# The hidden layer of batches 2 to 7 by seven block products, and attention beside the out layer

## The chip, the cores and the metric

One core of one Trainium2 chip runs the kernel. The metric is device time in microseconds (us); the median of three runs of the kernel before is 381.51 us (381.17 to 381.83). TensorE is called PE here, VectorE DVE, ScalarE ACT, GpSimd POOL and SyncE SP, as in the profile.

## What is computed

```
q, k, v: [8 batches, 12 heads, 448 rows, 64]
scores = q @ k^T / 8 - log(448);  attn = sigmoid(scores);  y = attn @ v
x = y with the heads side by side: [8*448, 768]
h = x @ w_in          (w_in  [768, 2048])
g = h * sigmoid(h)    (this is silu)
out = g @ w_out       (w_out [2048, 768]), float32 [3584, 768]
```

## The kernel before

Matmuls take float16 and add up in PSUM; q, k, v and the weights are cast by POOL's loads.

**Attention.** A *quad* `g` holds four heads of a batch, so a batch is three quads and there are 24. A quad has seven *chunks*; a `(g, ch)` pair is a unit, 168 in all (`units`). `scores` (L169) issues four 64x64 matmuls into a `pssc` tile, and one ACT sigmoid over 128x896 writes `attnT`. There are two `pssc` tiles of two PSUM banks each. `values` (L193) multiplies a quad's seven `attnT` tiles by v (seven *rounds* of four matmuls) and DVE writes the two halves into `xT[b]`, scaled by 64.

**Hidden layer.** `h_unit(b, fc)` (L229) is six matmuls of 448 columns for one of 16 blocks of 128 hidden columns; ACT takes the sigmoid and DVE multiplies, into `gTr`, which holds two batches side by side.

**Out layer.** `out_set` (L288) makes the rows of two blocks of 128 columns of `gTr` by a seven-product scheme: seven `product`s of eight matmuls of 384 columns, with sums of weights `tw[1]` to `tw[4]` (made once by `w_sums`, 16 subtractions of 128x768 on DVE, L277) and sums of `gTr` blocks `sg` (DVE, L318 to L327). In order the products read `wq[0][0]`, `wq[1][0]`, `tw[3]`, `tw[2]`, `tw[4]`, `tw[1]`, `wq[1][1]`. A pair of batches has three sets; every second pair has a fourth, made of the seventh block of this pair and of the one before (`kept`).

**PSUM banks.** All other PSUM tiles (`ph`, `po`, `pav`, `ptr`) share the tag `ps1` with four banks. A new tile gets, of the banks that are free at its place in the program, the one that was given back first.

**Order.** The order of instructions is written out by hand. `all_moe` is one generator of matmul steps for the hidden and the out layer, `stream`. The loop at the end (L541) issues two units of scores (a *burst*), a quad's values if any wait, and then calls `stretch(ns)`, which draws that many nanoseconds (189 for a hidden matmul, 163 for an out matmul) from the stream. So PE's queue holds bursts and stretches in turn. Up to unit 41 the stretches are 1,600 ns; at unit 42 there is one of 21,500 ns, in which h of batch 1 ends, and after that 2,000 to 3,400 ns. The last sets and h of batch 7 run after attention has ended.

**Queues.** POOL's queue holds the loads in order of the program: `load("kq", g)` is four DMAs, `load("v", g)` two. `after_values(g)` issues `v` of quad g+3, and others; quad 2 issues v 5, the last halves of `w_out`, kq 6 and kq 7; `transposes(4, "q")` issues kq 8; quad 5 issues kq 9. From quad 6 on, `dma_transpose` (L158) copies rows of k and q into `kr` and `qr` (ACT or DVE) and SP transposes them by DMA; the stores of the results are on SP too. For quads 6, 7, 8 `by_h1` puts these copies behind blocks 3, 6, 9 of h of batch 1, on ACT.

Of the kernel before, what the change touches and what calls it, by code (L numbers as in the profile page):

```python
# [2 lines left out]

# [14 lines left out]
def kernel(  # L18
# [14 lines left out]
    P = 128  # L33
# [88 lines left out]

    def new_qkT(g):
        for name in ("k", "q"):
            qkT[name, g] = p4.tile([P, NCH, P], F16, tag=f"{name}T", name=f"{name}T")

    dummy = cpool.tile([P, 512], F16, tag="dummy", name="dummy")

# [29 lines left out]
    def dma_transpose(g, name, copy):  # L158
        if ("k", g) not in qkT:
            new_qkT(g)  # L160
        rows = p3.tile([P, NCH, 2, D], F16, tag=f"{name}r", name=f"{name}r")
        copy(rows, flat[name, g].rearrange("p j c d -> p c j d"))  # L162
        nc.sync.dma_start_transpose(
            out=qkT[name, g], in_=rows.rearrange("p c j d -> p (c j d)")
        )
# [27 lines left out]
    def values(g, end=NCH):  # L193
        b, iq = divmod(g, NQ)
        if b not in xT:
            assert b < 2 or b - 2 in h_done
            xT[b] = p2.tile([P, NPAIR, S], F16, tag="xT", name="xT")
        pav, done_rounds = part_of.pop(g, None) or (
            [ps_1.tile([P, 512], F32, tag="ps1", name="pav") for _ in range(2)],
            0,  # L200
        )
        for ch in range(done_rounds, end):
            at = attnT.pop((g, ch))
            for half in range(2):
                own = slice(half * HP, (half + 1) * HP)
                for j in range(2):
                    nc.tensor.matmul(  # L207
                        pav[half][j * D : (j + 1) * D, :S],
                        flat["v", g][own, j, ch, :],
                        at[own, j, :],  # L210
                        start=(ch == 0),
                        stop=(ch == NCH - 1),
                    )
        if end < NCH:
            part_of[g] = pav, end
            return
        for half in range(2):
            nc.vector.tensor_scalar_mul(xT[b][:, half * NQ + iq, :], pav[half][:, :S], SX)  # L218
        if iq == NQ - 1:
            ready.add(b)  # L220

# [7 lines left out]
    def h_unit(b, fc):  # L229
        nonlocal hold  # L230
        hold = b > 0 and fc == NFC - 1
        ph = ps_1.tile([P, 512], F32, tag="ps1", name="ph")
        for at, cc in enumerate(pairs):
            assert b in ready or at < 4
            nc.tensor.matmul(  # L235
                ph[:, :S],
                w_in_sb[:, cc, fc * P : (fc + 1) * P],
                xT[b][:, cc, :],
                start=(at == 0),
                stop=(at == NCC - 1),  # L240
            )
            if at < NCC - 1:
                yield 189
        if fc == NFC - 1:
            h_done.add(b)
        tsig = p3.tile([P, S], F16, tag="tsig", name="tsig")
        nc.scalar.activation(tsig, ph[:, :S], AF.Sigmoid, bias=0.0, scale=ISX)  # L247
        nc.vector.tensor_mul(  # L248
            gTr[:, fc, (b % 2) * S : (b % 2) * S + S], ph[:, :S], tsig
        )  # L250
        yield 189

    rows_of = out.rearrange("(b p c) e -> b c p e", b=B, c=NCH)

# [11 lines left out]
    def w_sums():  # L266
        for i in (2, 3, 4):
            tw[i] = cpool.tile([P, NHC, NO2], F16, tag=f"T{i}", name=f"T{i}")
        tw[1] = wq[0][1]
        for o, x, y in (  # L270
            (tw[3], wq[1][1], wq[0][1]),
            (tw[1], wq[0][1], wq[0][0]),
            (tw[2], wq[1][1], tw[1]),
            (tw[4], tw[2], wq[1][0]),
        ):
            for f in range(0, NHC, 2):
                nc.vector.tensor_sub(o[:, f : f + 2], x[:, f : f + 2], y[:, f : f + 2])  # L277
                yield

    kept = cpool.tile([P, NFC, P], F16, tag="kept", name="kept")  # L280
# [4 lines left out]
    def row_blocks(m, g):  # L285
        return [rows_of[2 * m + u // NCH, u % NCH] for u in (2 * g, 2 * g + 1)]

    def out_set(a1, rows1, a2, rows2, last=False):  # L288
        nonlocal hold
        lo, hi = slice(0, NHC), slice(NHC, NFC)  # L290
        osb = [p4.tile([P, DMODEL], F32, tag="osb", name="osb") for _ in range(2)]
        c11, c12 = (osb[0][:, nh * NO2 : (nh + 1) * NO2] for nh in range(2))
        c21, c22 = (osb[1][:, nh * NO2 : (nh + 1) * NO2] for nh in range(2))
        m1 = p2.tile([P, NO2], F32, tag="m1", name="m1")
        sg = [cpool.tile([P, NHC, P], F16, tag=f"S{i}", name=f"S{i}") for i in range(1, 5)]

        def store(rows, o, cols, engines):
            for at, (row, eng) in enumerate(zip(rows, engines)):
# [1 line left out]

        left, right, whole = slice(0, NO2), slice(NO2, DMODEL), slice(0, DMODEL)

        def product(a, w):
            po = ps_1.tile([P, 512], F32, tag="ps1", name="po")
            for fc in range(NHC):
                nc.tensor.matmul(  # L306
                    po[:, :NO2], a[:, fc, :], w[:, fc, :], start=(fc == 0), stop=(fc == NHC - 1)
                )
                if fc < NHC - 1:
                    yield 163  # L310
            return po[:, :NO2]

        def plus(o, po, x, sign=ISX):
            nc.vector.scalar_tensor_tensor(  # L314
                out=o, in0=po, scalar=sign, in1=x, op0=ALU.mult, op1=ALU.add
            )

        nc.vector.tensor_sub(sg[2], a1[:, lo], a2[:, lo])  # L318
        nc.vector.tensor_add(sg[0], a2[:, lo], a2[:, hi])
        po = yield from product(a1[:, lo], wq[0][0])  # L320
        nc.scalar.activation(m1, po, AF.Copy, scale=ISX)  # L321
        nc.vector.tensor_sub(sg[1], sg[0], a1[:, lo])
        hold = False
        yield 163
        po = yield from product(a1[:, hi], wq[1][0])
        plus(c11, po, m1)
        nc.vector.tensor_sub(sg[3], a1[:, hi], sg[1])  # L327
        if last:
            store(rows1, osb[0], left, (nc.sync, nc.sync))
        yield 163  # L330
        po = yield from product(sg[2], tw[3])
        plus(c22, po, m1)
        yield 163
        po = yield from product(sg[1], tw[2])
        plus(c22, po, c22)
        plus(c12, po, m1)
        yield 163
        po = yield from product(a2[:, hi], tw[4])
        plus(c21, po, c22, -ISX)
        yield 163  # L340
        po = yield from product(sg[0], tw[1])
        plus(c22, po, c22)
# [9 lines left out]
        yield 163  # L352


    by_h1 = {3: 6, 6: 7, 9: 8}
    early = [h_unit(0, fc) for fc in range(2)]
    sums = w_sums()

    def moe_h(b):
        for fc in range(NFC):  # L360
            yield from early[fc] if b == 0 and fc < 2 else h_unit(b, fc)
            if b == 1:
                if fc >= 2:
                    next(sums)
                if fc in by_h1:
                    for name in ("k", "q"):
                        dma_transpose(by_h1[fc], name, act_copy)

    def moe_set(m, g):
        step = out_set(block(g), row_blocks(m, g), block(g + 1), row_blocks(m, g + 1))  # L370
        for i, ns in enumerate(step):
            if m % 2 == 0 and g == 2 and i % 8 == 4 and i < 32:
                fcs = slice(i // 8 * 4, i // 8 * 4 + 4)
                nc.scalar.activation(kept[:, fcs], block(NCH - 1)[:, fcs], AF.Copy)
            if m == 0 and g == 0 and i in (10, 14):
                next(sums)
            yield ns

    def all_moe():
        for m in range(B // 2):  # L380
            yield from moe_h(2 * m)
            if m > 0:
                yield from moe_set(m, 0)
            yield from moe_h(2 * m + 1)
            if m == 0:
                yield from moe_set(m, 0)
            yield from moe_set(m, 2)
            yield from moe_set(m, 4)
            if m % 2 == 1:
                g = NCH - 1  # L390
                yield from out_set(
                    kept, row_blocks(m - 1, g), block(g), row_blocks(m, g), m == B // 2 - 1
                )

    stream = all_moe()
# [44 lines left out]
    def after_values(g):  # L440
# [18 lines left out]
                load("kq", to)  # L459
        if g == 5:  # L460
            load("kq", 9)
        if g >= 6 and g + 3 < NQB:
            later.extend(((g + 3, "k"), (g + 3, "q")))

    later = []

    def rows_if_any():
        if later:
            g, name = later.pop(0)
            dma_transpose(g, name, nc.vector.tensor_copy)  # L470
            if name == "q" and g + 4 < NQB and g + 4 > 12:
                load("kq", g + 4)

    def values_if_any():
        if waiting:
            g = waiting.pop(0)
            values(g)
            after_values(g)

    keep_busy(9)  # L480
    pe_transpose(
# [54 lines left out]
        for do, *what in behind.get(n, ()):  # L536
            do(*what)

    paces = {1: 1600, 2: 2000, 3: 2550, 4: 3400, 5: 3400, 6: 3000, 7: 3000}
    stretch(paces[1])  # L540
    for n in range(NT_B + 3, len(units), 2):  # L541
        burst = units[n : n + 2]
        if n == 2 * NT_B:
            values_if_any()
            stretch(21500)
        for u in burst:
            scores(*u)
        values_if_any()
        rows_if_any()
        for g, ch in burst:  # L550
            if ch == NCH - 1:
                waiting.append(g)
        if n in (24, 30):
            transposes(4 + (n - 24) // 6, "k")
        elif n in (26, 32):
            transposes(4 + (n - 26) // 6, "q")
        stretch(paces[1] if 1 not in ready else paces[n // NT_B])
    for g in waiting:
        values(g)
    for _ in stream:  # L560
        pass

# [29 lines left out]
```

## Time and profile before

| | before |
|---|---|
| median of 3 runs | 381.51 us (381.17 to 381.83) |
| the profiled execution | 381.95 us, its span 380.2 us |
| PE busy | 370.8 us, 98% of the span |
| DVE, ACT, POOL busy | 235.2, 225.9, 93.5 us |
| granted TensorE clock | 1.000 |
| hidden matmuls (L235) | 768 |
| out matmuls (L306) | 784 |
| units of scores (L183) | 168, 918 ns each on ACT |

Durations are of the one profiled execution; start times count from the start of its span. "Idle before" is the time in which the engine stood still before an instruction, and what ended it. A matmul's duration contains its latency; what one costs in a row is the distance from start to start, so a group's start and the next group's start give the price.

### The profile page before, as it was taken

How to read it: one execution, taken by the hardware profiler on the slowest of the kernel's cores; microseconds unless marked ns; L12 is line 12 of the kernel's file. 1: busy time of each engine (PE TensorE's matmuls, PEld its weight loads, DVE VectorE, ACT ScalarE, POOL GpSimd, SP SyncE). 2: the span in 40 equal slices, each digit the busy share in tenths (PEclk: the TensorE clock that was granted, in tenths of full speed). 3: DMA queues.
4: the chain of work that ended last, by engine and by line, in shares of the span. 5: the costliest groups of instructions: out<-in, count | busy, mean ns of one | idle time of the engine just before them, and what ended most of it. 6: DMA issues, size and time to landing. Idle time of an engine off the chain costs nothing.

```text
span 380.2 us, 7666 instructions
## 1 busy us (share of the span) xinstructions
PE 370.8 (98%) x3083; PEld 186.0 (49%) x3083; DVE 235.2 (62%) x416; ACT 225.9 (59%) x329; POOL 93.5 (25%) x158
## 2 busy tenths in 40 slices
PE   7989999999999999999999999999999999999995
PEld 2444445545554445445555444544455444555563
DVE  2636646987565666566766647735757446656773
ACT  4988875757667764777434576477764776054000
POOL 8946325403752323122221303101100000000000
PEclk9999999999999999999999999999999999999999
DMA  7999999995999947945939949536347300110233
GB/s 125 177 185 204 205 204 171 133 140 110 165 241 216 151 56 99 173 54 69 162 67 183 132 78 121 71 86 74 48 85 97 84 3 2 50 34 0 82 85 83
DMA packets 66403, 42.80 MB, mean 113 GB/s; under 512 B 37056, under 2 KB 62912, under 8 KB 66368
## 3 DMA queue, kind: packets, MB, share of 16 engines
q0 software_dynamic: 28032, 22.59, 43.2%
q1 hardware_dynamic: 38112, 19.41, 28.5%
q8 instruction: 24, 0.39, 0.4%
q10 hardware_dynamic: 224, 0.33, 0.3%
q14 instruction: 11, 0.09, 0.1%
HBM read 45.61 MB, written 11.01 MB: 149 GB/s over the span
## 4 chain that ended last, share of the span: by engine, by line
PE 78%; DMA 13%; POOL 3%; DVE 3%; ACT 2%; issue 1%; ACTq 0%; POOLq 0%
PE po L306 34%; PE ph L235 29%; PE psc L176 8%; PE pav L207 6%; DMA w_in_sb<-in_moe_w_in_dram 5%; DMA w_out_sb<-in_moe_w_out_dram 5%; DMA qf<-in_q_dram 1%; DMA vf<-in_v_dram 1%; POOL kf L78 1%; DVE gTr L248 1%; DVE T L277 1%; POOL qf L78 1%; ACT qr L137 1%; POOL vf L78 1%; ACT attnT L183 0%
## 5 line engine op out<-in xcount | busy, mean ns | idle before, releaser
L183 ACT ACTIVATE attnT<-psc 128x896 f16<-128x896 f32 x168 | 144.2, 918 | 59.9 <-PE psc L176 59.8
L235 PE MATMUL ph<-xT,w_in_sb 128*128 128x448 f16 x768 | 153.2, 353 | 1.2 <-DMA w_in_sb<-in_moe_w_in_dram 1.2
L248 DVE TENSOR_TENSOR gTr<-ph,tsig 128x448 f16<-128x448 f32 x128 | 78.9, 623 | 70.1 <-ACT tsig L247 68.6
L235 PEld LDWEIGHTS <-w_in_sb 128*128 128x128 f16 x768 | 71.9, 98 | 77.1 <-issue 12.8
L247 ACT ACTIVATE tsig<-ph 128x448 f16<-128x448 f32 x128 | 68.6, 547 | 54.4 <-PE ph L235 53.7
L78 POOL DMA_DIRECT2D vf<-in_v_dram x48 | 28.9, 624 | 136.4 <-PE pav L207 136.4
L306 PEld LDWEIGHTS <-S 128*128 128x128 f16 x448 | 42.3, 98 | 33.9 <-issue 6.8
L314 DVE SCALAR_TENSOR_TENSOR osb<-po,osb 128x384 f32<-128x384 f32 x70 | 37.6, 554 | 25.2 <-PE po L306 24.5
L176 PE MATMUL psc<-qT,kT 64*64 64x448 f16 x672 | 50.7, 362 | 0.9 <-ACT attnT L183 0.3
L218 DVE TENSOR_SCALAR xT<-pav 128x448 f16<-128x448 f32 x48 | 27.7, 619 | 31.4 <-PE pav L207 31.4
L306 PE MATMUL po<-T,S 128*128 128x384 f16 x224 | 40.6, 327 | 0.1
L306 PEld LDWEIGHTS <-gTr 128*128 128x128 f16 x304 | 28.7, 98 | 23.4 <-issue 5.0
L306 PE MATMUL po<-w_out_sb,S 128*128 128x384 f16 x224 | 39.9, 326 | 0.0
L207 PE MATMUL pav<-attnT,vf 64*64 64x448 f16 x672 | 37.5, 349 | 0.2 <-DVE gTr L248 0.2
L78 POOL DMA_DIRECT2D qf<-in_q_dram x46 | 27.7, 613 | 39.4 <-DVE qr L162 16.7
L306 PE MATMUL po<-w_out_sb,gTr 128*128 128x384 f16 x192 | 34.7, 327 | 0.0
L78 POOL DMA_DIRECT2D kf<-in_k_dram x50 | 30.3, 618 | 7.8 <-DVE kr L162 4.3
L176 PEld LDWEIGHTS <-kT 64*64 64x64 f16 x672 | 14.2, 104 | 31.0 <-issue 29.0
L207 PEld LDWEIGHTS <-vf 64*64 64x64 f16 x672 | 20.1, 107 | 12.3 <-issue 1.5
L314 DVE SCALAR_TENSOR_TENSOR osb<-po,m 128x384 f32<-128x384 f32 x42 | 23.1, 551 | 3.9 <-PE po L306 2.5
L306 PE MATMUL po<-T,gTr 128*128 128x384 f16 x112 | 21.4, 326 | 0.0
L321 ACT ACTIVATE m<-po 128x384 f32<-128x384 f32 x14 | 6.9, 492 | 24.0 <-PE po L306 24.0
(41 smaller groups left out, 130.8 us busy)
## 6 DMA issues: line engine op xcount, KB each, us to landing
out_dram<-osb SPq DMA_DIRECT2D x54, 192.0 KB, 3.0
vf<-in_v_dram POOLq DMA_DIRECT2D x48, 112.0 KB, 4.4
kf<-in_k_dram POOLq DMA_DIRECT2D x46, 112.0 KB, 5.4
qf<-in_q_dram POOLq DMA_DIRECT2D x46, 112.0 KB, 5.8
w_in_sb<-in_moe_w_in_dram POOLq DMA_DIRECT2D x4, 768.0 KB, 10.6
w_out_sb<-in_moe_w_out_dram POOLq DMA_DIRECT2D x4, 768.0 KB, 17.1
kT<-kr SPq DMA_TRANSPOSE x18, 5.8
qT<-qr SPq DMA_TRANSPOSE x18, 5.6
```

The lines of the kernel that those rows point to most:

```text
L78: nc.gpsimd.dma_start(flat[name, g][half * HP : (half + 1) * HP, :, c0:c1].rearrange("p i c d -> p i (c d)"), source[name][b, h0 : h0 + 2] ...
L137: nc.scalar.activation(o, i, AF.Copy)
L176: nc.tensor.matmul(psc[own, j, :S], qkT["k", g][rows, ch, own], qkT["q", g][rows, :, own], start=True, stop=True,)
L183: nc.scalar.activation(attnT[g, ch], psc[:, :, :S], AF.Sigmoid, bias=NEG_LOG_S, scale=QKSCALE)
L207: nc.tensor.matmul(pav[half][j * D : (j + 1) * D, :S], flat["v", g][own, j, ch, :], at[own, j, :], start=(ch == 0), stop=(ch == NCH - 1),)
L218: nc.vector.tensor_scalar_mul(xT[b][:, half * NQ + iq, :], pav[half][:, :S], SX)
L235: nc.tensor.matmul(ph[:, :S], w_in_sb[:, cc, fc * P : (fc + 1) * P], xT[b][:, cc, :], start=(at == 0), stop=(at == NCC - 1),)
L247: nc.scalar.activation(tsig, ph[:, :S], AF.Sigmoid, bias=0.0, scale=ISX)
L248: nc.vector.tensor_mul(gTr[:, fc, (b % 2) * S : (b % 2) * S + S], ph[:, :S], tsig)
L306: nc.tensor.matmul(po[:, :NO2], a[:, fc, :], w[:, fc, :], start=(fc == 0), stop=(fc == NHC - 1))
L314: nc.vector.scalar_tensor_tensor(out=o, in0=po, scalar=sign, in1=x, op0=ALU.mult, op1=ALU.add)
L321: nc.scalar.activation(m1, po, AF.Copy, scale=ISX)
```

## The change

For batches 2 to 7 the hidden layer is made per pair of batches (`h_pair`). The two batches' `xT`, each cut into two halves of 384 rows, and `w_in`, cut into four blocks, are multiplied by a scheme of seven block products of three matmuls per 128 hidden columns, in place of eight. For each `i` of eight, products 1 and 2 add up in the bank `xb`, 6, 7 and 4 in `y` (a `pssc` tile), 5 and 3 in `z`; ACT copies product 1 out (`p1`), DVE adds (`u2`, `u3`, `p1`), and ACT takes one `Silu` per sum into `gTr`. Products 3 and 4 of block `i` run inside block `i+1` (`late`). The sums of `w_in` (`w_in_sums`: nine of 128x1024 drawn during h of batch 0, three more in the second out set) and the sums of `w_out` (`w_sums`, 16 of 128x768, drawn during h of batch 1) are made on POOL; the sums of `xT` (`x_sums`) on DVE. Batches 0 and 1 keep `h_unit`.

All units of scores of the next pair are issued in the out layer's time of the pair before; `h_pair` runs with no scores. `Silu` and `Sigmoid` are called on one element (`warm`) where they change. The first set of a later pair does the rest of the last block inside its first product, and reads `tw[3]` second. Buffers: `qkT` 3 (was 4), `rows` 2 (was 3), `osb` 3 (was 4). `gTr` of batches 2 to 7 holds silu itself, so the out sets' factor there is 1.

```
...
-        rows = p3.tile([P, NCH, 2, D], F16, tag=f"{name}r", name=f"{name}r")
+        rows = p2.tile([P, NCH, 2, D], F16, tag=f"{name}r", name=f"{name}r")
...
+            if b > 2 and b % 2 == 1 and iq == NQ - 1 and half == 0:
+                nc.scalar.activation(
+                    xT[b][:, half * NQ + iq, :], pav[half][:, :S], AF.Copy, scale=SX
+                )
...
+        if b > 2 and b % 2 == 1:
+            x_sums(b // 2, iq)
...
+    def x_sums(m, iq):
...
+        for o, x, y in ((t1, b12, b11), (t2, b22, t1), (t4, b21, t2), (t3, b22, b12)):
+            nc.vector.tensor_sub(o, x, y)
...
+    def w_in_sums():
...
+        for c in range(HCC):
+            nc.gpsimd.tensor_add(sw[1][:, c], a21[:, c], a22[:, c])
+            yield
+            nc.gpsimd.tensor_sub(sw[2][:, c], sw[1][:, c], a11[:, c])
+            yield
+            nc.gpsimd.tensor_sub(sw[4][:, c], a12[:, c], sw[2][:, c])
+            yield
+        for c in range(HCC):
+            nc.gpsimd.tensor_sub(sw[3][:, c], a11[:, c], a21[:, c])
+            yield
...
+        def product(n, ps, i, first):
+            a, bs = sides[n]
+            for c in range(HCC):
+                nc.tensor.matmul(
...
+        def late(i, y, z, p1, u2, u3):
+            silu(1, 1, i, u3)
+            if m < B // 2 - 1 and i < 4:
+                rows_of_quad(2 * NQ * (m + 1) + 1 + i // 2, "kq"[i % 2], act_copy)
+            yield from product(3, z, i, False)
+            nc.vector.tensor_add(u2, z, u2)
+            silu(0, 1, i, u2)
+            yield from product(4, y, i, False)
+            nc.vector.tensor_add(p1, y, p1)
+            silu(1, 0, i, p1)
...
+        def begin(i):
+            xb = ps_1.tile([P, 512], F32, tag="ps1", name="hx")[:, :S]
+            yield from product(1, xb, i, True)
+            p1 = p3.tile([P, S], F32, tag="m1", name="p1")
+            nc.scalar.activation(p1, xb, AF.Copy)
...
+        yield from begin(0)
+        for i in range(NHC):
+            end = i == NHC - 1
+            if not end:
+                yield from begin(i + 1)
+            xb, p1 = begun[i]
+            y = ps_sc.tile([P, 2, 512], F32, tag="pssc", name="hy")[:, 0, :S]
+            yield from product(6, y, i, True)
+            u2 = p3.tile([P, DMODEL], F32, tag="osb", name="u2")[:, :S]
+            nc.vector.tensor_add(u2, y, p1)
...
+            z = ps_1.tile([P, 512], F32, tag="ps1", name="hz")[:, :S]
+            yield from product(5, z, i, True)
+            if behind is not None and not end:
+                yield from late(*behind)
+            yield from product(2, xb, i, False)
+            silu(0, 0, i, xb)
+            yield from product(7, y, i, False)
...
+            nc.vector.tensor_add(u3, y, p1)
...
+                nc.vector.tensor_add(u3, z, u3)
...
             for f in range(0, NHC, 2):
-                nc.vector.tensor_sub(o[:, f : f + 2], x[:, f : f + 2], y[:, f : f + 2])
+                nc.gpsimd.tensor_sub(o[:, f : f + 2], x[:, f : f + 2], y[:, f : f + 2])
                 yield
...
-        osb = [p4.tile([P, DMODEL], F32, tag="osb", name="osb") for _ in range(2)]
+        osb = [p3.tile([P, DMODEL], F32, tag="osb", name="osb") for _ in range(2)]
...
+        po = yield from product(a1[:, lo], wq[0][0], between)
...
+        if tail:
+            po = yield from product(sg[2], tw[3])
...
-    by_h1 = {3: 6, 6: 7, 9: 8}
+    by_h1 = {0: 6, 4: 7, 8: 8}
...
             yield from early[fc] if b == 0 and fc < 2 else h_unit(b, fc)
+            if b == 0 and fc >= 7:
+                next(in_sums)
             if b == 1:
-                if fc >= 2:
-                    next(sums)
+                next(sums)
...
-                nc.scalar.activation(kept[:, fcs], block(NCH - 1)[:, fcs], AF.Copy)
-            if m == 0 and g == 0 and i in (10, 14):
-                next(sums)
+                nc.vector.tensor_scalar_mul(kept[:, fcs], block(NCH - 1)[:, fcs], scale)
+            if m == 0 and g == 2 and i in (36, 44, 52):
+                next(in_sums)
...
+                yield from h_pair(m, tail)
+            yield from moe_set(m, 0, tail)
...
-    paces = {1: 1600, 2: 2000, 3: 2550, 4: 3400, 5: 3400, 6: 3000, 7: 3000}
...
+    PACE, BURST, ROUND, SPARE = 1600, 590, 200, 2400
+    sets = 7 * NHC * 163
+    h_at = [(2 * NFC * NCC - 8) * 189 + 3 * sets]
+    for m in (1, 2):
+        h_at.append(h_at[-1] + 7 * NHC * HCC * 189 + (3 + m % 2) * sets)
+    AHEAD = 4
+    ends = [2 * NT_B, 4 * NT_B + AHEAD, 6 * NT_B + AHEAD, 8 * NT_B]
...
             values_if_any()
-            stretch(21500)
+            stretch(12500)
...
+        dense = h_at[m - 1] - SPARE - done
+        due = done
+        stretch((dense + values_left * ROUND) / ((ends[m] - n) // 2) - had * ROUND)
+        values_left -= had
+        if n + 2 == ends[m]:
+            while waiting:
+                values_if_any()
+                stretch(SPARE / 3)
+            values_left = 2 * NT_B
+            while 2 * m not in h_done:
+                done += next(stream)
+            due = done
+            stretch(3000)
...
```

## The prediction

> **What bounds the kernel now.** The page comes first, for PE's share.
>
> ```profile
> span 380.2 us, 7666 instructions
> ...
> PE 370.8 (98%) x3083; PEld 186.0 (49%) x3083; DVE 235.2 (62%) x416; ACT 225.9 (59%) x329; POOL 93.5 (25%) x158
> ...
> PE   7989999999999999999999999999999999999995
> ...
> PE 78%; DMA 13%; POOL 3%; DVE 3%; ACT 2%; issue 1%; ACTq 0%; POOLq 0%
> ```
>
> PE is busy in every slice from the fourth on, and the chain that ended last is PE's. A matmul removed is time removed, and a wait put before PE is time added: nothing later can take it up. The timeline of PE gives the prices and the places that matter.
>
> ```profile
> 57.39 18.90 PE L235 MATMUL ph<-xT,w_in_sb 128*128 128x448 f16 x99
> 76.12 2.76 PE L306 MATMUL po<-w_out_sb,gTr 128*128 128x384 f16 x16
> ...
> 330.17 18.32 PE L235 MATMUL ph<-xT,w_in_sb 128*128 128x448 f16 x96
> 348.33 2.76 PE L306 MATMUL po<-w_out_sb,gTr 128*128 128x384 f16 x16
> ```
>
> 96 hidden matmuls start 18.16 us apart from the next group: 0.189 us each (an out matmul, 0.163). The same view gives 0.25 us for a unit's scores and 0.204 for a round of values. The groups by line give the rest.
>
> ```profile
> L183 ACT ACTIVATE attnT<-psc 128x896 f16<-128x896 f32 x168 | 144.2, 918 | 59.9 <-PE psc L176 59.8
> ...
> L247 ACT ACTIVATE tsig<-ph 128x448 f16<-128x448 f32 x128 | 68.6, 547 | 54.4 <-PE ph L235 53.7
> ...
> L319 DVE TENSOR_TENSOR S<-gTr 128x1024 f16<-128x1024 f16 x14 | 9.6, 683 | 0.0
> ...
> L277 DVE TENSOR_TENSOR T<-w_out_sb 128x768 f16<-128x768 f16 x8 | 4.4, 548 | 0.0
> ...
> masks.py:199 POOL TENSOR_SCALAR_AFFINE_SELECT ident<-ident 128x128 f16<-128x128 f16 x1 | 0.3, 288 | 0.1
> ...
> masks.py:197 POOL MEMSET ident<- 128x128 f16 x1 | 0.2, 243 | 0.0
> ```
>
> POOL has no operation on two tensors here; these two rows of 128x128 are the nearest, and memsets of one element take 99 to 102 ns. Last, POOL's own timeline, for when it is free.
>
> ```profile
> 57.30 0.59 POOL L78 DMA_DIRECT2D qf<-in_q_dram  x1 [3.04 <-DMA w_out_sb<-in_moe_w_out_dram]
> 61.15 0.59 POOL L78 DMA_DIRECT2D qf<-in_q_dram  x1 [3.27 <-DMA w_out_sb<-in_moe_w_out_dram]
> 62.04 1.18 POOL L78 DMA_DIRECT2D kf<-in_k_dram  x2 [0.30 <-issue]
> 63.20 1.21 POOL L78 DMA_DIRECT2D qf<-in_q_dram  x2
> 64.37 3.60 POOL L78 DMA_DIRECT2D vf<-in_v_dram  x6
> ```
>
> POOL runs 20 us behind the program: kq 6, issued behind values of quad 2, begins at 44.3, and the q loads wait for w_out. kq 8 ends at 64.4, v 6 (a third of the last line) at 65.6.
>
> **What is taken away.** A pair of batches cost 192 hidden matmuls and costs 168: 3 x 24 = 72 fewer, 72 x 0.189 = **13.6 us**. Scores, values and out matmuls keep their numbers. The 96 sigmoids and multiplications of those batches go too, but neither engine bounds.
>
> **The scheme's own work.** A block is 21 matmuls, 3.97 us. ACT has one copy and four silus of 448, 0.54 each and 0.43 from start to start where two stand in a row, at half of the blocks a 0.94 us copy of rows: at most 3.7. DVE has five adds (nearest row the 0.62 us multiplication, 0.54 start to start): 2.7 to 3.1. PE stays last. Banks: block i+2 begins right behind product 7 of block i. Two banks can be free then, that of `z` of block i-1, given back by DVE after product 3, and that of `xb` of block i, given back by the silu after product 2, which stands behind the adds and silus of product 4. The first is given back first, so it is taken: no wait, and `xb`'s bank goes to `z` 1.13 us later. I take 0; the other bank is a rival below.
>
> **Attention in the out layer's time.** In a stretch of three sets PE has 27.3 us of products, 10.5 of scores and 8.6 of values, 46.4; ACT has 42 x 0.81 (start to start) = 34 and 1.5 of `m1`. A burst costs PE 2.06 to 2.35 us and ACT 1.62. PE stays the bound: 0. At the seams: the last values of a pair, then 0.2 to DVE, 0.62 for `xT`, three sums of 448 (by the slope between the 548 and 683 ns rows 0.38 each): 2.0 us, beside about 1.6 us of out matmuls and two products 1 (1.1). Covered; if the adds of the set are in front of them, up to 0.4. A table load is 1.28 us (the one row, ACT's first call) and there are six, where ACT has nothing urgent. One microsecond for all seams, 0 to 4.
>
> **The sums on POOL.** This decides. Before, DVE made the 16 sums of w_out between 62.7 and 81.1, and out set 0 found them ready. Now they are in POOL's queue. In order of the program it holds kq 8, v 6, four sums of w_in, v 7, four more, v 8 and kq 9, the ninth, and then the 16: h of batch 0 draws eight before unit 42, and the load behind unit 42 stands before the ninth. POOL waits for no PE there, so from 65.6 it has eight loads of 0.6 (4.8 us), nine sums of 1024 and 16 of 768. The last sum is ready at 70.4 + 9a + 16b.
>
> Price of a sum: a memset costs (243 - 101)/127 = 1.12 ns per element for one written stream, the select (288 - 101)/128 = 1.46 for one read and one written, both over 0.1 us. Bounds for a second read: hidden, 1.46; as dear as a stream, 2.58. As POOL's own rows are nearer than DVE's (0.55 us for 768), I take the middle, 2.0: a = 2.15, b = 1.64, and the last sum at 70.4 + 19.4 + 26.2 = 116.0. By 1.46 it is 104.3, by 2.58 128.4.
>
> When PE wants it: from 57.39, 12,500 ns are 66 matmuls, to 69.9. The other 33 (6.2) with four bursts of scores (0.5 each) end at 78.1. `tw[4]`, last in POOL's queue, is read by the fifth product of set 0: 40 matmuls (6.5), five bursts (2.5), 14 rounds of values (2.8) later it would end, at 89.9. It can end at 116.0 + 0.3 (its last two matmuls). So PE waits **26.4 us**, first at the third product (`tw[3]`, wanted at 83, ready at 96), then at the fourth and fifth; bounds 14.7 and 38.8. Behind the waiting matmul stand the rest of set 0, every later burst and the whole stream, and DVE, ACT and the stores starve behind PE. POOL's later loads (v 9, kq 10 to 12) stand behind the sums and are not wanted before PE moves again; kq 9 is issued at 85 instead of 68 and the copy of its rows holds DVE, but within the same wait.
>
> The Trainium skill, "GPSIMD Engine Reference", section 3.1, advises VectorE for elementwise work and gives 4497 ns for a two-input sum of 2048 float32, 2.2 ns per element. By that a and b would be 2.25 and 1.69 and the sum 1.7 us longer; no run here shows it. The skill's "SBUF — State Buffer", section "Who interferes with whom", says that a VectorE instruction with two SBUF inputs and a GpSimd instruction reading SBUF lock each other out. By that the four `sg` sums of set 0 would hold POOL up 0.68 us each, 2.7 more; in this trace POOL has no such instruction, so it is untested.
>
> Also early: scores of quad 6 are asked for at 69.9, before at 79.2. Its q rows are transposed on SP at 65.5 in a crowded time:
>
> ```profile
> qT<-qr SPq DMA_TRANSPOSE x1, 12.5
> ```
>
> That is 78.0, eight microseconds late; at the usual 5.6, one. It lies inside POOL's wait, and costs 1 to 8 only if that cover is gone.
>
> **Sum.** 381.95 (profiled execution) - 13.6 + 26.4 + 1 = 395.8. The median stands 0.44 under the profiled execution: **395.4**. With the bounds of the sums and seams: 383 to 411.
>
> **Rivals.** *POOL is quick.* If its sums cost what DVE's do (0.68 and 0.55), the last is ready at 85.3 and PE doesn't wait for it. Then 381.5 - 13.6 + 1 plus 1 to 8 for quad 6's transposes: 370 to 377, say 374. It decides from 1.36 ns per element, where the wait eats the gain; at the memset's 1.12 the wait is 7.4 and the result 376. For it: the select may be slow for its own reasons, and the rows are short. Against: 1.12 is already a stream without any read. Faster, 30%.
>
> *The scheme waits for its own silu, POOL being quick.* If block i+2 takes `xb`'s bank, it waits behind product 4 for 0.20 + 0.62 (add) + 0.44 + 0.54 (two silus) = 1.8 us, with 1.1 of PE work beside: 0.7 us, five times a pair, 10.5 in all. 374 + 10.5 - 4 (the transposes' middle) = 380 to 385. Order of release speaks against. 6%.
>
> *ACT bounds the attention stretches.* From about 1.05 us per unit ACT would be later than PE; the row says 0.81 in a row. Some 5 us per pair, 15 on top of the quick case: about 389. 4%.
>
> **How the numbers follow.** Forecast 60%, rivals 30, 6 and 4. Runs of this kernel spread by 0.33 us to either side, so 0.2% (0.8 us) is what can be told from no change. Faster 31% (the quick case and a part of the second), same 3%, slower 66%. The likeliest case alone reaches from 383 to 408 (over 408 only with the dearest rows); as both signs hold much, the range takes in the quick case too, from 372.
>
> **What would show it.** Right: POOL rows of 128x768 at about 1.6 us, the last near 116; PE idle in out set 0, released by POOL sums, 20 us or more; 768 - 72 = 696 hidden matmuls; PE without gaps in the pairs. Wrong: sums under 1.1 us, or a set 0 that runs through. A gap of 0.7 us at each block of a pair would be the second rival, ACT without idle in the out sets the third.

## The result, and the profile after

| | before | after |
|---|---|---|
| median | 381.54 us (381.17 to 381.83, 4 runs) | 407.92 us (407.50 to 410.59, 4 runs) |
| the profiled execution, its span | 381.95, 380.2 | 407.74, 406.0 |
| PE, DVE, ACT, POOL busy, us | 370.8, 235.2, 225.9, 93.5 | 365.0, 277.1, 253.8, 144.8 |
| mean granted TensorE clock | 1.000 | 0.960 |
| hidden matmuls | 768 | 696 (192 at L243, 504 at L309) |

The changed kernel takes 1.0707 times as long, 95% interval 1.0660 to 1.0753: 26.4 us more, where 13.9 had been forecast. Its page, the lines that answer to those shown of before:

```profile
span 406.0 us, 7668 instructions
...
PE 365.0 (90%) x3011; PEld 181.5 (45%) x3011; DVE 277.1 (68%) x463; ACT 253.8 (63%) x368; POOL 144.8 (36%) x186
...
PE   7999998934379839999999999999999999999995
...
PEclk9999999978579969999999999999999999999998
...
PE 61%; DMA 18%; POOL 15%; issue 3%; DVE 2%; SPq 0%; DVEq 0%; POOLq 0%
```

A slice is 10.15 us. PE's holes lie in slices 7 to 15, from 61 to 152 us, nearly all of them from slice 9 on; behind them it is full until the last slice. POOL, 3% of the chain before, is 15% now. PE's timeline (start, duration, line, tiles; in brackets the idle time ahead of it and what ended it) names the holes:

```profile
90.46 0.80 PE L457 MATMUL po<-T,S 128*128 128x384 f16 x2 [6.98 <-POOL T L426]
...
103.19 0.80 PE L457 MATMUL po<-T,S 128*128 128x384 f16 x2 [6.30 <-POOL T L426]
...
114.36 2.74 PE L457 MATMUL po<-T,gTr 128*128 128x384 f16 x8 [5.54 <-DVE xT L224]
...
148.36 0.59 PE L177 MATMUL psc<-qT,kT 64*64 64x448 f16 x4 [6.45 <-DMA qT<-qr]
```

The first two are the forecast wait for POOL's sums; POOL's timeline has them at the forecast price:

```profile
64.47 2.19 POOL L283 TENSOR_TENSOR W<-w_in_sb 128x1024 f16<-128x1024 f16 x1
...
88.78 6.40 POOL L426 TENSOR_TENSOR T<-w_out_sb 128x768 f16<-128x768 f16 x4
...
107.89 6.84 POOL L426 TENSOR_TENSOR T<-T,w_out_sb 128x768 f16<-128x768 f16 x4
```

Four sums start 6.37 us after the four before them, 1.59 each, and the last ends at 114.7; 1.64 and 116.0 had been forecast. The third hole is released by DVE, which is no slower at `xT` than before. DVE's timeline shows why it came late:

```profile
86.76 0.55 DVE L467 SCALAR_TENSOR_TENSOR osb<-po,m 128x384 f32<-128x384 f32 x1
87.23 26.02 DVE L487 TENSOR_TENSOR S<-gTr,S 128x1024 f16<-128x1024 f16 x1
```

One sum of two tiles in SBUF, 0.68 us elsewhere, lasts 26.02 us, to 113.25: it stands beside POOL's ninth sum of w_in and 15 of the 16 of w_out, and gets through only ahead of the last. In the groups by line (busy us, mean ns; then the idle time ahead and what ended most of it) it makes the row of 12 such sums 34.5 us, in place of 8.2:

```profile
L457 PE MATMUL po<-T,S 128*128 128x384 f16 x224 | 44.0, 335 | 15.8 <-POOL T L426 15.8
...
L487 DVE TENSOR_TENSOR S<-gTr,S 128x1024 f16<-128x1024 f16 x12 | 34.5, 2877 | 0.0
...
L320 ACT ACTIVATE gTr<-u 128x448 f16<-128x448 f32 x48 | 27.6, 575 | 19.4 <-DVE u L329 14.8
...
L426 POOL TENSOR_TENSOR T<-w_out_sb 128x768 f16<-128x768 f16 x8 | 12.8, 1624 | 0.0
```

By the first of these rows PE stood still 15.8 us for POOL's sums, where the prediction had named 20 or more as the sign of being right; the 5.54 us for `xT` come on top. The fourth hole, 6.45 us, lies 34 us behind POOL's last sum of w_out: the transposed q of quad 11, issued at 131.8, is there at 148.3.

### The profile page after: what moved, and what is told of

Read it like the earlier page. It is cut to its first block, busy times and chain, and to the rows that moved or that the text cites. A ratio compares the mean times of both kernels' runs of the same rounds, so it can differ in the third digit from the quotient of the medians.

```text
span 406.0 us, 7668 instructions
## 1 busy us (share of the span) xinstructions
PE 365.0 (90%) x3011; PEld 181.5 (45%) x3011; DVE 277.1 (68%) x463; ACT 253.8 (63%) x368; POOL 144.8 (36%) x186
## 4 chain that ended last, share of the span: by engine, by line
PE 61%; DMA 18%; POOL 15%; issue 3%; DVE 2%; SPq 0%; DVEq 0%; POOLq 0%
PE po L457 28%; PE hy L309 10%; PE hx L309 7%; PE hz L309 7%; PE psc L177 6%; DMA w_in_sb<-in_moe_w_in_dram 6%; PE pav L208 5%; DMA w_out_sb<-in_moe_w_out_dram 4%; POOL T L426 4%; DMA qT<-qr 4%; POOL kf L79 2%; POOL W L287 2%; POOL W L285 2%; POOL W L283 2%; POOL vf L79 1%
## 5 line engine op out<-in xcount | busy, mean ns | idle before, releaser
L457 PE MATMUL po<-T,S 128*128 128x384 f16 x224 | 44.0, 335 | 15.8 <-POOL T L426 15.8
L208 PE MATMUL pav<-attnT,vf 64*64 64x448 f16 x672 | 42.1, 354 | 1.6 <-DVE osb L467 1.3
L243 PE MATMUL ph<-xT,w_in_sb 128*128 128x448 f16 x192 | 39.2, 353 | 1.7 <-DVE gTr L256 1.7
L309 PEld LDWEIGHTS <-w_in_sb 128*128 128x128 f16 x288 | 28.2, 98 | 26.4 <-issue 0.4
L320 ACT ACTIVATE gTr<-u 128x448 f16<-128x448 f32 x48 | 27.6, 575 | 19.4 <-DVE u L329 14.8
L457 PE MATMUL po<-w_out_sb,gTr 128*128 128x384 f16 x192 | 37.4, 334 | 0.6 <-DVE xT L224 0.6
L309 PE MATMUL hy<-xs,w_in_sb 128*128 128x448 f16 x144 | 35.1, 352 | 0.1
L256 DVE TENSOR_TENSOR gTr<-ph,tsig 128x448 f16<-128x448 f32 x32 | 19.0, 621 | 23.6 <-ACT tsig L255 23.5
L309 PE MATMUL hx<-xT,w_in_sb 128*128 128x448 f16 x144 | 34.6, 352 | 0.0
L487 DVE TENSOR_TENSOR S<-gTr,S 128x1024 f16<-128x1024 f16 x12 | 34.5, 2877 | 0.0
```

What stands on the lines that cost most here:

```text
L208: nc.tensor.matmul(pav[half][j * D : (j + 1) * D, :S], flat["v", g][own, j, ch, :], at[own, j, :], start=(ch == 0), stop=(ch == NCH - 1),)
L243: nc.tensor.matmul(ph[:, :S], w_in_sb[:, cc, fc * P : (fc + 1) * P], xT[b][:, cc, :], start=(at == 0), stop=(at == NCC - 1),)
L256: nc.vector.tensor_mul(gTr[:, fc, (b % 2) * S : (b % 2) * S + S], ph[:, :S], tsig)
L309: nc.tensor.matmul(ps, a[:, c, i * P : (i + 1) * P], bs(c), start=(first and c == 0), stop=(c == HCC - 1), skip_group_check=True,)
L320: nc.scalar.activation(gTr[:, side * NHC + i, odd * S : (odd + 1) * S], src, AF.Silu, scale=ISX)
L457: nc.tensor.matmul(po[:, :NO2], a[:, fc, :], w[:, fc, :], start=(fc == 0), stop=(fc == NHC - 1))
```

## The experiments

Two theories of the 26.4 us were open from here on: PE waits for sums (the prediction's), or DVE stands still while POOL works; and beside both, attention of the next pair isn't fed in time.

### POOL's sums

**All 28 sums on DVE.** `nc.gpsimd` becomes `nc.vector` in `w_in_sums` and `w_sums`:

```
-            nc.gpsimd.tensor_add(sw[1][:, c], a21[:, c], a22[:, c])
+            nc.vector.tensor_add(sw[1][:, c], a21[:, c], a22[:, c])
...
```

> The changed kernel with all 28 weight sums (16 of w_out, 12 of w_in) on DVE in the places where POOL had them. Theory (POOL's price and queue order cost the time): no wait for sums in out set 0, sums of 0.55 and 0.68 us, POOL's loads on time, so the second wait (6.5 us at the transposed q of quad 11) goes too: 381.5 - 13.6 + 1 to 6 for quad 6's late loads and the seams = 369 to 374 us. Rival (the seven-product scheme and the crowded attention lose the time themselves): over 385 us, with PE gaps that have nothing to do with sums.

Measured: 383.96 us (381.74 to 385.55), 1.0052 times before (1.0021 to 1.0082). POOL's sums, with what stands behind them in its queue, cost 24.0 us of the changed kernel. But the scheme's gain doesn't appear: both expectations are missed, and PE still has holes:

```profile
64.55 6.40 PE L243 MATMUL ph<-xT,w_in_sb 128*128 128x448 f16 x33 [1.90 <-DVE gTr L256]
...
73.57 0.57 PE L177 MATMUL psc<-qT,kT 64*64 64x448 f16 x8 [2.63 <-DMA qT<-qr]
...
122.63 0.59 PE L177 MATMUL psc<-qT,kT 64*64 64x448 f16 x4 [6.64 <-DMA qT<-qr]
```

**The sums of w_in later on POOL**, so that those of w_out come early; with w_out's on DVE (first), and with both on POOL (second):

```
-            if b == 0 and fc >= 7:
-                next(in_sums)
...
-            if m == 0 and g == 2 and i in (36, 44, 52):
-                next(in_sums)
+            if m == 0 and g >= 2 and i % 9 == 4:
+                next(in_sums, None)
```

> The changed kernel with the w_out sums on DVE as before, and the twelve w_in sums still on POOL but drawn in the second and third out set of batches 0 and 1, where nothing waits for them soon. Theory: 370 to 378 us; POOL's 2.13 us sums cost only where they hold a DVE instruction with two SBUF inputs (its S sums would show up to 2.1 us longer) or a load. Rival (any sum on POOL spoils the out layer, by DVE held up): over 385 us.

> The changed kernel with both kinds of sums on POOL, but the twelve w_in sums drawn in the second and third out set, so the w_out sums are not behind nine of them. Theory (queue arithmetic): first w_out sum at 64.5 + 4.8 of loads = 69.4, the last at 69.4 + 16 x 1.61 = 95.1, wanted by PE's fifth product for an end at 88.7, so 6 to 8 us of wait in place of 28: 376 to 386 us. Rival (DVE locked out by POOL, not the late sums, made the wait): DVE is still held for as long as POOL sums run in a row, and the time stays near 395.

Measured: 400.64 us (398.68 to 402.77), ratio 1.0505 (1.0462 to 1.0547), and 416.84 us (413.84 to 418.14), ratio 1.0920 (1.0862 to 1.0978). Nobody waits for the 12 moved sums so early; they cost 16.7 us against the all-DVE kernel all the same. From the DVE timeline of the first of the two, and then POOL's:

```profile
130.62 6.04 DVE L472 TENSOR_TENSOR S<-gTr 128x1024 f16<-128x1024 f16 x1
```

```profile
133.92 2.17 POOL L283 TENSOR_TENSOR W<-w_in_sb 128x1024 f16<-128x1024 f16 x1
136.17 2.46 POOL L285 TENSOR_TENSOR W<-W,w_in_sb 128x1024 f16<-128x1024 f16 x1
```

DVE's sum gets through in the pause of 0.08 us ahead of the second of these, which reads what the first wrote.

In the second kernel, w_out's last sum was done at 100.5 instead of 114.7, and it became slower still: a DVE sum stood still for 14.10 us beside w_out's, and four more for 4.82 to 6.41 beside w_in's. A queue's arithmetic, from which the forecast was made, can't give that.

**The kernel before, with w_out's 16 sums on POOL** (the line in `w_sums` alone), and **the kernel before, with 16 sums more on POOL that nobody reads**:

```
+    idle = cpool.tile([P, 2, NO2], F16, tag="idle", name="idle")
...
+                nc.gpsimd.tensor_sub(idle, w_in_sb[:, 0:2, :NO2], w_in_sb[:, 2:4, :NO2])
```

> The kernel before with one part of the change alone: the 16 w_out sums on POOL. Theory: POOL is through v 8 and kq 9 at 73.1, sums of 1.61 end at 98.9, the fifth product of set 0 ended at 84.1: 15 us of wait, 393 to 400 us. If only the combination with w_in sums or the scheme hurts: 381 to 385.

> The kernel before, its own 16 w_out sums left on DVE, plus 16 sums of 128x768 on POOL that read w_in and that nobody reads, queued where the POOL sums of the one-part kernel were. No instruction depends on them, so late sums can't hold PE. Theory (a DVE sum of two SBUF tensors can't start while POOL works through sums in a row): one DVE sum of some 20 us, PE idle behind it, 395 to 402 us. Rival (only sums that come late cost time): 381 to 383 us.

Measured: 404.28 us (403.28 to 405.45), ratio 1.0600 (1.0574 to 1.0626), and 394.76 us (393.55 to 397.31), ratio 1.0349 (1.0313 to 1.0385). So sums that nobody waits for cost 13.3 us, though not by the one DVE sum of some 20 us that had been expected. DVE's timeline of the first, and PE's only hole there:

```profile
76.70 21.70 DVE L318 TENSOR_TENSOR S<-gTr 128x1024 f16<-128x1024 f16 x1
```

```profile
98.45 0.50 PE L306 MATMUL po<-T,S 128*128 128x384 f16 x1 [20.31 <-DVE S L318]
```

DVE's timeline of the second, where POOL's 16 sums took 30.59 us, 1.91 each and not 1.59:

```profile
83.10 2.11 DVE L326 TENSOR_TENSOR S<-gTr 128x1024 f16<-128x1024 f16 x1
85.14 2.12 DVE L327 TENSOR_TENSOR S<-gTr 128x1024 f16<-128x1024 f16 x1
87.29 2.01 DVE L330 TENSOR_TENSOR S<-S,gTr 128x1024 f16<-128x1024 f16 x1
```

DVE's sums wait out one POOL sum each, 2.1 us for 0.68; PE lost 5.77 us behind the first of the three, and later 3.7 us in three waits for transposed q. Two of POOL's sums in the second, the upper beside a DVE sum of two SBUF tiles, the lower beside none:

```profile
84.75 1.96 POOL L285 TENSOR_TENSOR idle<-w_in_sb 128x768 f16<-128x768 f16 x1
...
96.74 1.65 POOL L285 TENSOR_TENSOR idle<-w_in_sb 128x768 f16<-128x768 f16 x1
```

So 1.91 is in the main what DVE's sums do to POOL's, and not why DVE got in. What differs ahead of that is small: each of these sums writes the tile of the one before, and POOL pauses 0.08 us between them; w_out's sums don't depend on their neighbours, and each starts 0.03 us before the end of the one before. In the traces of the changed kernel and of the five others with POOL sums here, a DVE sum stood ready at 17 places where POOL paused 0.08 us between two sums, and got through at all of them (13 in this kernel, four in the two with w_in's sums later); at 61 places where POOL's sums overlapped, it got through at two. That the pause lets DVE in is the reading that fits; no run changed it alone.

**The changed kernel, with w_out's sums on POOL unread**: as it is, but the 16 sums go to a tile that nobody reads and the products take w_out as loaded, so this kernel leaves the sums out of its result.

```
-            (tw[3], wq[1][1], wq[0][1]),
...
+            (idle, wq[1][1], wq[0][1]),
...
+        tw.update({1: wq[0][1], 2: wq[1][1], 3: wq[1][1], 4: wq[1][0]})
```

> The changed kernel with the 16 sums of w_out still worked out on POOL, but written to a tile that nobody reads; the out layers' products read w_out as it was loaded (the sums are left out of the computation). No product waits for a sum any more. Theory (DVE's sums of g with two operands in SBUF stand still as long as POOL's sums follow one another without a gap, so PE still waits for them in out set 0): the time stays near the changed kernel's, 400 to 408 us, with a DVE instruction of 20 us or more in the trace. Rival (the prediction's term: PE's wait was for the last sum): that wait goes, 384 to 390 us, and no DVE instruction is longer than two of POOL's sums, some 4 us. Between them: DVE gets in between two sums and each of its instructions takes some 2 us, as in the kernel before with unread sums, 390 to 397 us.

Measured: 410.34 us (408.87 to 412.16), ratio 1.0766 (1.0734 to 1.0799): nothing is won, and the time lies 2 us above the range of the theory that fits. DVE's timeline and then PE's:

```profile
87.43 27.59 DVE L486 TENSOR_TENSOR S<-gTr,S 128x1024 f16<-128x1024 f16 x1
```

```profile
116.13 2.72 PE L456 MATMUL po<-w_out_sb,gTr 128*128 128x384 f16 x8 [26.30 <-DVE xT L224]
```

POOL's sums ran from 88.99 to 114.46. With no sum to wait for, PE stands still once in out set 0, for 26.30 us, for an `xT` that is queued on DVE behind the held sum. The wait of the prediction is real, but a second one of the same length and the same end lies over it, and taking away the first alone saves nothing; no run takes away the second alone. Between this kernel and the all-DVE one lie 26.4 us, and no sum of w_out that is waited for is among them.

### Feeding the attention

All of these start from the all-DVE kernel, whose time is as long as that of before though it has 72 matmuls less.

**Loads or start times spread.** Quads 10, 11, 12 loaded one at a time; quad 6 asked for 4.5 us later; both.

```
-        if g == 6:
-            for to in (10, 11, 12):
-                load("kq", to)
+        if g in (6, 7, 8):
+            load("kq", g + 4)
```

```
-    by_h1 = {0: 6, 4: 7, 8: 8}
+    by_h1 = {3: 6, 6: 7, 9: 8}
...
-            stretch(12500)
+            stretch(17000)
```

> The kernel with all sums on DVE, and the loads of q and k of quads 10, 11, 12 issued one quad at a time (behind values of quads 6, 7, 8) in place of all three behind quad 6. Theory (the transposes of quad 11 land late because they share the DMA engines with that pile of loads): the 6.6 us wait shrinks or goes, 375 to 380 us. Rival (the transposes are slow for another reason, such as the stores on SP, or asked for too late): the wait stays, 382 to 386.

> The kernel with all sums on DVE, with the row copies of quads 6, 7, 8 back behind blocks 3, 6, 9 of h of batch 1 and 17,000 ns of h (changed kernel: 12,500) before the scores of quad 6. Theory: the waits of 1.9 us (ACT held by a load) and 2.6 us (transposed q of quad 6) go, the later wait stays or grows a little: 379 to 382 us. Rival (these waits only move into the bursts): no change, 382 to 386.

> Both of the last two together. Theory: all three waits gone or small, PE works 13.6 us less than before and waits 1 to 3 more: 369 to 374 us, faster than the kernel before. Rival (the attention of batches 2 and 3 can't be fed in the out layer's time): over 378.

Measured: 384.84 us (382.36 to 388.79), 387.72 (385.97 to 390.39), 386.87 (383.44 to 388.91); ratios 1.0077 (1.0052 to 1.0103), 1.0179 (1.0137 to 1.0222), 1.0127 (1.0086 to 1.0167). None helps: the first and third came out as their rivals had it, the second above both of its ranges. The waits moved: with spread loads, a row copy on DVE waited for the load, and PE lost 3.53 us to `osb` behind it; with the later start, 4.39 us on `gTr` and 4.38 on `qT`.

**Nothing to feed.** The q and k of quads 6 to 11 are neither loaded nor copied nor transposed; their scores read those of quad 5, so this kernel leaves a part of the computation out:

```
+            if name != "v" and 6 <= g < 12:
+                continue
...
+        if 6 <= g < 12:
+            qkT[name, g] = qkT[name, 5]
+            return
```

> All 28 weight sums on DVE as in the all-DVE kernel, and the q and k of quads 6 to 11 (batches 2 and 3) are neither loaded nor copied to rows nor transposed: their scores read the transposed q and k of quad 5 (that part of the computation is left out). Theory (the scheme does save its 72 matmuls, and what eats the gain is the feeding of pair 1's attention): the three PE waits of the all-DVE kernel's trace go, 1.90 + 2.63 + 6.64 us, and the matmuls at low clock behind the last of them, some 1.7 us: 384.0 - 12.9 = 371 us, range 368 to 374. Rival (the loss is spread over the scheme's own short instructions and seams): the waits go elsewhere and the time stays above 379 us.

Measured: 368.48 us (368.28 to 369.62), ratio 0.9660 (0.9626 to 0.9693). The scheme is worth 13.0 us, and feeding the second pair's attention costs 383.96 - 368.48 = 15.5. Over the whole stretch in question (columns: window, its length, then busy time of PE, PEld, DVE, ACT, POOL with counts, clock, DMA share, GB/s) PE has no hole left:

```profile
56.00:164.00 108.00, 107.78 (x852) 53.21 (x844) 82.00 (x156) 79.81 (x119) 24.98 (x42) 1.00 0.53 88
```

**The loads earlier.** In the all-DVE kernel v of quad 9 stood ahead of kq 10 to 12 in POOL's queue and waited 15.6 us for its buffer. So kq 9, 10, 11 go out in batch 1's h layer, as soon as their own buffers are free, and 12 to 16 behind the values of quads 8 to 11; and in a second kernel, kq 6 ahead of w_out's right half, with the sums of w_out two at a time:

```
                         dma_transpose(by_h1[fc], name, act_copy)
+                    load("kq", by_h1[fc] + 3)
...
-        if g == 6:
-            for to in (10, 11, 12):
-                load("kq", to)
...
+        if 8 <= g < 12:
+            load("kq", g + 4)
```

```
+            load("kq", 6)
             load_w_out(1, 0)
             load_w_out(1, 1)
-            load("kq", 6)
...
+                if 6 <= fc < 14:
+                    next(sums)
+                    next(sums)
```

> The all-DVE kernel with the loads of the later quads moved: q and k of quads 9, 10 and 11 go out in batch 1's h layer, each behind the transposes of quads 6, 7 and 8, in the stretch at 66 to 90 us where the DMA engines were at 6 tenths and less; those of 12 to 16 behind the values of quads 8 to 11 and not beside the transposes of 10 and 11. Theory (quad 11's transposes landed 13 to 15 us after issue since six loads lay beside them): the 6.64 us wait and the low clock behind it go, the 1.90 and 2.63 us at quad 6 stay: 384.0 - 8.3 = 375.7, range 374 to 379, some 1.5% under the kernel before. Rival (the loads now meet w_out's and the transposes of 7 and 8, or DVE is held by another row copy): the wait moves, 382 to 387 us as in the three kernels that only spread loads or pace.

> The kernel with the earlier loads, and q and k of quad 6 also go out ahead of the right half of w_out; the 16 sums of w_out follow two at a time behind units 6 to 13 of batch 1's h layer instead of one behind each. Theory: quad 6's wait (2.63 us) goes and DVE is no longer held by w_out's landing (1.90 us): 375.7 - 4.5 = 371 us, range 369 to 376. Rival (w_out's right half now lands after its sums are queued on DVE, and PE waits for h sums behind them): a wait on DVE of 2 to 6 us in batch 1's h layer, 377 to 383 us.

Measured: 377.67 us (376.68 to 379.26), ratio 0.9898 (0.9861 to 0.9935), and 380.78 us (377.96 to 381.90), ratio 0.9969 (0.9947 to 0.9991). The first is as expected: the 6.64 us wait is gone. The second came out in its rival's range, by another wait: quad 6's transposes were issued 1.8 us earlier but met w_out's load, and PE waited 7.57 us for them in place of 2.40. What was left in the first kernel shows in DVE's timeline: DVE stood still ahead of a row copy (the trace names no releaser), and PE behind it for 1.74 us.

```profile
112.61 0.62 DVE L163 COPY kr<-kf 128x896 f16<-128x896 f16 x1 [4.59 <-issue]
```

**Tuned.** From the first of the two: kq 12 also goes out in batch 1's h layer, kq 9 to 11 four units later than there, and v 7 and v 8 behind units 8 and 12.

```
-                    load("kq", by_h1[fc] + 3)
+                if fc in (8, 12):
+                    load("v", 5 + fc // 4)
+                if fc in (4, 8, 12):
+                    load("kq", 8 + fc // 4)
+                if fc == 12:
+                    load("kq", 12)
...
-            load("kq", g + 4)
...
+            load("kq", g + 5)
```

> The kernel with the earlier loads, with three moves more: q and k of quad 12 go out behind batch 1's h unit 12, so that DVE isn't held at 107 to 112 us by the row copy that waits for them (PE's 1.74 and 0.69 us there); those of 9, 10, 11 each four units later and v of quads 7 and 8 behind units 8 and 12, so that the transposes of quad 6 have fewer loads beside them (PE's 2.40 us). Theory: 377.7 less 2 to 5 us, 372.5 to 376. Rival (quad 6 is late since its own load lands behind w_out, and the other waits move to the next load): 376.5 to 379 us.

Measured: 374.32 us (373.45 to 377.57), ratio 0.9831 (0.9801 to 0.9861). This version beats both kernels, by 7.0 and 33.6 us. The throughput by slice (GB/s), of the all-DVE kernel and of this one:

```profile
GB/s 125 177 188 204 205 204 179 154 105 80 181 223 126 157 107 127 120 5 0 127 210 193 210 48 122 84 24 2 98 135 155 2 84 0 0 3 63 97 90 83
```

```profile
GB/s 127 175 186 204 205 204 175 141 161 139 157 166 218 126 169 119 58 0 67 188 186 180 162 65 117 76 2 0 138 125 134 2 86 0 0 3 84 87 85 85
```

The low at 76 to 95 us and the crowd behind it (105, 80, then 181, 223) have become even (161, 139, 157, 166). In the crowd a transposition took 14 to 15 us to land, in the all-DVE kernel's own DMA view from 104 to 125 us:

```profile
qT<-qr SPq DMA_TRANSPOSE x2, 15.2
```

In the same window of the kernel before it was 9.9, beside 25 loads and stores against 20 here, so their number alone doesn't set it; what else does is open. The kernel before spread the scores of quads 6 to 11 over 64.5 us (79.2 to 143.7); the tuned one has them in 48.5 (73.8 to 122.2) and so has less time for the same loads. What stays in the tuned kernel, 1.57 us on `gTr` and 2.36 on quad 6's `qT` at 65 and 74 us, is most of the 5.8 us to the kernel with nothing to feed.

## Why the prediction was wrong

| step of the prediction | forecast | measured | from |
|---|---|---|---|
| 72 matmuls less, seams | -13.6 + 1 = -12.6 | -13.0 | nothing to feed, against before |
| sums on POOL | +26.4 | +24.0 | changed kernel, against all sums on DVE |
| feeding quads 6 to 11 | 0, "inside POOL's wait" | +15.5 | all sums on DVE, against nothing to feed |
| together | +13.9 | +26.4 | changed kernel, against before |

The three steps are taken one on top of the other, so that they add up is no check, and in another order each share could differ.

**The scheme.** Right, to half a microsecond. In the changed kernel `h_pair` runs without a hole from 164.5 us on, in groups of three matmuls 0.57 apart. So two rivals fall: no block waits for its own silu, and ACT, though its silus from SBUF took 0.575 us where 0.54 had been taken, doesn't bound the attention stretches: with nothing to feed PE is busy for 107.78 of 108 us there, ACT for 79.8.

**The price of a sum on POOL.** Right: 2.12 for 1024 and 1.59 for 768, against 2.15 and 1.64. The rival of a quick POOL falls with it. The Trainium skill's figure ("GPSIMD Engine Reference", section 3.1), 2.2 ns per element for float32, lies 6% over the 2.07 measured here in float16.

**What the sums cost.** The size came out, by luck; the mechanism was half of it. The step that failed here is the sentence on the lock: it counted what DVE's sums would hold POOL up (four of 0.68 us) and not what POOL's sums would hold DVE up. That is the large side: 26.02 us in the changed kernel, 21.70 in the one before with w_out's sums on POOL, 27.59 where nobody read them. In the changed kernel both waits end within 1.5 us (POOL's last sum 114.7, DVE's 113.25), and so the sum came out near. In the kernel with both kinds of sums on POOL and w_in's later, the same arithmetic of the queue gave 376 to 386 us, and it took 416.8. The Trainium skill, "SBUF — State Buffer", section "SBUF: two separate sides", has this in both directions: whichever of the two instructions starts first keeps the shared ports "for the whole instruction", and the other blocks. The traces agree on who is stopped: the instruction at 86.76 above, with one input in PSUM, took its usual 0.55 beside a sum on POOL. They differ on for how long: DVE's sum stood still not for one of POOL's but for 14 to 16 in a row, where these followed without a pause.

**The feeding.** Not a size that was off but a step that was missing, and the one that the number lacked: the forecast put the feeding of the next pair's attention at nothing beside POOL's wait, and with all sums on DVE it measured 15.5 us. "POOL's later loads [...] are not wanted before PE moves again" is true and no help: when PE moved, at 117 us, v 9 and kq 10 to 12 went out only then (114.7 on), beside the transposes of quads 9 to 11, and PE stood still for quad 11 at 142 to 148, outside the wait that was to cover it. The prediction weighed the landing of quad 6 alone, and the change shortens the time of all six quads. The page of before had a sign of it, the DMA engines at 9 tenths for much of the first 130 us:

```profile
DMA  7999999995999947945939949536347300110233
```

**The clock.** Not in the sum. With PE idle the granted clock was 0.83 from 80 to 100 us, 0.57 from 100 to 120 and 0.83 from 140 to 160. Behind the holes at 114 and 148, 8 and 10 out matmuls took 2.74 and 2.96 us; before, 1.46 and 1.79: 2.5 us for these two groups.

## What to carry to other kernels

Before moving elementwise work to an idle POOL, list DVE's instructions with two inputs in SBUF that fall into the same time. Count the first as standing still for the whole run of POOL's where these don't depend on each other (21.7 to 27.6 us here), and each as waiting out one of them where every one depends on the one before (2.1 us here). Sums that nobody waits for can cost as much as awaited ones. Work that is squeezed into a shorter time needs its loads and transposes squeezed too: check the DMA row of the profile and the order of each queue for every buffer of that work, not only for the first one. And when two waits may end at the same place, try to take away each alone and both: that a forecast's size comes out doesn't show its mechanism.

## What the runs showed of the hardware

- A DVE sum of two SBUF tiles (128x1024, 0.68 us by itself) lasted 21.7 to 27.6 us where it met sums of 128x768 on POOL that followed one another without a pause (14 to 16 of them), and 2.1 us where POOL paused 0.08 us between two. POOL's sum pays as well: 1.96 us beside such a DVE sum, 1.65 beside none.
- Some DVE sums stood still while POOL's timeline still shows loads being issued ahead of a sum: 2.70 us at 84.14 in the changed kernel. Others beside such loads took their 0.68; why is open.
- Four DMA transposes of the all-DVE kernel, issued between 104 and 125 us beside 20 loads and stores, landed after 14.2 (k) and 15.2 us (q, medians of two each); the medians of all are 4.1 and 6.5 there. In the kernel before, beside 25 in the same window, three landed after 7.1 and 9.9.
- In the changed kernel's stretch from 100 to 120 us PE worked 9.7 of 20 us; the mean granted clock over it was 0.57, and 8 matmuls at 114.36, behind 5.54 us of idle time, took 2.74 us, where 8 such took 1.46 in the kernel before.
